# Weights in other pieces, on-chip copies of the sinks' v and other banks for four attention units, in a fused window-attention and gated-layer kernel

## The chip, the cores and the metric

The kernel runs on one core of a Trainium2 chip. Its five engines work side by side, each through its own list of instructions in order: TensorE (PE) multiplies matrices into PSUM, VectorE (DVE) and ScalarE (ACT) work elementwise, GpSimd (POOL) makes masks, casts and issues DMAs with a cast, SyncE (SP) issues other DMAs. Semaphores order them against each other. The metric is the device time of one launch in microseconds (us), the median of several runs; less is better.

## The reference

Attention first: q, k, v of 4 batches x 8 heads x 768 positions x 64, float32. A query sees the keys of a causal window of 128 positions and, besides, the first 4 positions (the sinks):

```python
keep = is_sink | in_window            # pos < 4, or 0 <= query - key < 128
scores = where(keep, q @ k.T / 8, -1e9)
a = softmax(scores);  attn = a @ v    # -> x of 3072 tokens x 512
```

Then a layer with a gate: h = x @ w_in (512 x 2048), g = h * sigmoid(beta * h), out = g @ w_out (2048 x 512), float32, 3072 x 512.

## The kernel before

The 3072 tokens are cut into 8 tiles (T) of 384. A tile's x needs four **units** of attention: unit n is one pair of heads and half a sequence, n // 8 its batch, n % 4 its pair of heads, n // 4 % 2 its half. Units 0 to 3 make tile 0, units 4 to 7 tile 1, and so on. A unit of the second half (4 to 7 among them) reads keys and sinks of the first half too.

A unit goes through these steps: q and k are loaded by SP as float32 (`load_qk`, L522), cast by POOL (`cast`, L621) and transposed by PE into bank tr, from where ACT or DVE copies them into qkT (`transpose_in`, L634, L641). Scores of the sinks are one matmul (`scores_sink`, L670) and an exponential on ACT (L673); scores of the window come in two groups, a and b, each with an exponential over two banks (`scores`, L700, L707) and a product with a mask on DVE (`apply_mask`, L714). `attend` multiplies with v (L759 the sinks' v in `v_sink`, L770 the window's v in `v_aug`), `normalise` divides by the sum (L779, L781), `transpose_out` turns the result through PE (L798) into xT (L802). Units 0 to 3 have the same steps with banks of their own. From unit 12 on (XBAR), q, k and v are landed with a cast by POOL's DMAs (L552, L561) and transposed by DMAs of SP (L567, L790).

The layer: a tile has 16 **blocks** of 128 columns of h. A block is four matmuls with w_in (`hidden`, L814), a tanh on ACT (L822) and a gate on DVE (L835); `project` (L843) multiplies g with w_out, 48 matmuls of a tile, for three tokens' groups t and 16 rows m of w_out, accumulating in acc0 or acc1; then out_sb is copied and stored (L851, L859). In tile 0 the blocks rotate through four banks, acc1, h0, h1 and acc0 among them, afterwards through h0 and h1.

PSUM has eight banks: s0, s1, tr and av (s_ps), h0 and h1 (h_ps), acc0 and acc1. In units 4 to 7 the sink scores go to s0, group a to s0 and s1, group b to h0 and h1, `attend` to av, `transpose_out` through tr.

The weights are loaded with a cast by POOL's DMAs: w_in in four pieces of 1 MB (`load_w_in`, L578; 0.5 MB each once cast), w_out in eight pieces (`load_w_out`, L583), v of tile 1 in three pieces (`load_v`, L542). The first four rows of k and v of all batches are loaded by `load_sinks`: k_rows early (L592), v_sink after the masks (L596).

**The order.** Each step is a node with a cost, and a planner (`Prog`) orders every engine's nodes: it takes, again and again, the node that can start first by its costs and by a model of the DMA queues, of equals the one that stands earlier in the program. Banks and buffers are reused in the order of the program: a node that writes one waits for all earlier readers. The resulting list of each engine is fixed, and the chip runs it in order. In the program, the main loop over s emits blocks (s < 16 for tile 0, then a gap of 8 steps, then a block per step), the units' steps by AGENDA (units 4 to 7: `in` at s = 0 to 3, the others from s = 16 on), casts, loads and projections (none for s < 16, three per step in the gap).

## Time and profile before

| | us |
|---|---|
| median of 3 runs | 228.73 (228.01 to 229.79) |
| the profiled execution | 228.59 |
| its span, first to last instruction | 226.9 |
| PE busy | 220.0 |
| ACT, DVE, POOL busy | 141.3, 132.6, 125.7 |
| first block of tile 0, of tile 1, of tile 2 | 17.32, 44.51, 70.53 |
| first projection | 35.08 |

The span is that of the profiled execution; 1.7 us lie around it. Times in the text are from the span's start. Matmuls are pipelined: each row gives a duration with a modelled end, and the next one often starts before it. Under the engines' names stand the lines of the kernel. A DMA's time runs from its issue to the landing of its last byte.

### The profile page before, as it was taken

To read this page: it belongs to the slowest core of one execution; us is meant where nothing else is said; L and a number is where in the kernel's file an instruction comes from. 1 tells how busy PE (TensorE), PEld (TensorE's weight loads), DVE (VectorE), ACT (ScalarE), POOL (GpSimd) and SP (SyncE) were. 2 spreads that over 40 slices of the span, in tenths; PEclk is the share of its full clock that TensorE was granted. 3 is DMA by queue.
4 is the path that set the end of the run, shared out by engine and by line. 5 is a ranking of instruction groups with operands and counts; after the bars stand their busy time and mean duration, and the time that the engine had idled before them with its cause. 6 is when DMAs were issued, how large, how long until landed. Compare 5 with 4: busy or idle time off the path is not lost.

```text
span 226.9 us, 4463 instructions
## 1 busy us (share of the span) xinstructions
PE 220.0 (97%) x1761; PEld 122.1 (54%) x1761; DVE 132.6 (58%) x264; ACT 141.3 (62%) x224; POOL 125.7 (55%) x191
## 2 busy tenths in 40 slices
PE   7999989999999999999999999999999999999995
PEld 4665545555555555555555555555555555555454
DVE  5466777488975776566565656555656564443200
ACT  1877796197586877566657766666656755555311
POOL 4689992899994979695939396876300000000000
PEclk9999999999999999999999999999999999999999
DMA  6999999999998999999999999998921012110122
GB/s 172 251 172 179 276 194 205 257 228 139 118 138 124 124 117 151 120 167 144 116 113 135 99 138 147 96 165 119 94 80 53 20 57 64 49 46 0 58 83 92
DMA packets 96901, 28.92 MB, mean 127 GB/s; under 512 B 83424, under 2 KB 93936, under 8 KB 96880
## 3 DMA queue, kind: packets, MB, share of 16 engines
q0 software_dynamic: 59232, 10.92, 65.7%
q1 hardware_dynamic: 34304, 16.79, 34.3%
q10 hardware_dynamic: 3344, 0.93, 1.9%
q8 instruction: 14, 0.23, 0.5%
q14 instruction: 7, 0.06, 0.1%
HBM read 27.34 MB, written 6.29 MB: 148 GB/s over the span
## 4 chain that ended last, share of the span: by engine, by line
PE 73%; DMA 15%; POOL 8%; issue 2%; SPq 1%; ACT 0%; POOLq 0%; ACTq 0%
PE acc L843 32%; PE h_ps L814 29%; DMA k_stage<-in_k_dram 8%; DMA w_out<-in_moe_w_out_dram 4%; PE s_ps L727 4%; PE s_ps L770 4%; POOL qk L621 3%; DMA w_in<-in_moe_w_in_dram 2%; POOL land L552 2%; PE h_ps L843 2%; POOL v_aug L561 1%; PE s_ps L759 1%; PE s_ps L670 1%; SPq L522 1%; POOL v_aug L532 0%
## 5 line engine op out<-in xcount | busy, mean ns | idle before, releaser
L822 ACT ACTIVATE th<-h_ps,beta_half 128x384 f32<-128x384 f32 x120 | 69.4, 581 | 59.7 <-PE h_ps L814 59.1
L843 PE MATMUL acc<-w_out,g 128*128 128x512 bf16 x368 | 99.7, 380 | 0.0
L814 PE MATMUL h_ps<-xT,w_in 128*128 128x384 bf16 x480 | 96.2, 326 | 0.0
L835 DVE SCALAR_TENSOR_TENSOR g<-th,h_ps 128x384 bf16<-128x384 f32 x120 | 65.6, 550 | 44.8 <-ACT th L822 44.0
L814 PEld LDWEIGHTS h_ps<-xT,w_in 128*128 128x128 bf16 x480 | 45.6, 98 | 39.8 <-issue 0.8
L843 PEld LDWEIGHTS acc<-w_out,g 128*128 128x128 bf16 x368 | 32.8, 98 | 28.8 <-issue 3.6
L552 POOL DMA_DIRECT2D land<-in_q_dram x40 | 30.2, 760 | 24.0 <-DVE rden L779 24.0
L552 POOL DMA_DIRECT2D land<-in_k_dram x40 | 30.3, 761 | 0.0
L561 POOL DMA_DIRECT2D v_aug<-in_v_dram x40 | 30.2, 760 | 0.0
L735 ACT ACTIVATE E<-s_ps 128x1536 bf16<-128x1536 f32 x20 | 28.8, 1442 | 0.0
L741 DVE TENSOR_TENSOR E<-E,mask 128x1536 bf16<-128x1536 bf16 x20 | 19.2, 958 | 16.4 <-ACT E L735 16.4
L851 ACT ACTIVATE out_sb<-acc 128x512 f32<-128x512 f32 x23 | 13.7, 596 | 7.6 <-PE acc L843 7.4
L770 PEld LDWEIGHTS s_ps<-v_aug,E 128*128 128x128 bf16 x336 | 15.2, 97 | 3.2 <-issue 1.2
L770 PE MATMUL s_ps<-v_aug,E 128*128 128x65 bf16 x336 | 16.8, 193 | 0.0
L707 ACT ACTIVATE E<-s_ps 128x768 bf16<-128x768 f32 x17 | 13.7, 811 | 4.3 <-PE s_ps L700 4.2
L781 DVE TENSOR_TENSOR o_norm<-s_ps,rden 128x384 bf16<-128x384 f32 x28 | 15.6, 556 | 0.8
L714 DVE TENSOR_TENSOR E<-E,mask 128x768 bf16<-128x768 bf16 x16 | 9.0, 572 | 2.0 <-ACT E L707 1.3
L727 PE MATMUL s_ps<-qkT 64*128 64x256 bf16 (+2 forms) x144 | 10.1, 254 | 0.0
L759 PE MATMUL s_ps<-v_sink,E_sink 128*128 128x130 bf16 x48 | 9.3, 219 | 0.0
L621 POOL CAST qk<-k_stage 128x384 bf16<-128x384 f32 x12 | 6.5, 544 | 4.7 <-DMA k_stage<-in_k_dram 4.4
L673 ACT ACTIVATE E_sink<-s_ps 128x384 bf16<-128x384 f32 x16 | 7.8, 490 | 1.5 <-PE s_ps L670 1.5
L727 PEld LDWEIGHTS s_ps<-qkT 64*128 64x128 bf16 x144 | 4.9, 94 | 7.1 <-issue 5.8
(75 smaller groups left out, 155.2 us busy)
## 6 DMA issues: line engine op xcount, KB each, us to landing
out_dram<-out_sb SPq DMA_DIRECT2D x23, 256.0 KB, 2.7
q_stage<-in_q_dram SPq DMA_DIRECT2D x12, 192.0 KB, 7.4
k_stage<-in_k_dram SPq DMA_DIRECT2D x12, 192.0 KB, 7.9
w_in<-in_moe_w_in_dram POOLq DMA_DIRECT2D x4, 512.0 KB, 6.8
w_out<-in_moe_w_out_dram POOLq DMA_DIRECT2D x8, 256.0 KB, 9.6
land<-in_q_dram POOLq DMA_DIRECT2D x40, 48.0 KB, 3.7
land<-in_k_dram POOLq DMA_DIRECT2D x40, 48.0 KB, 4.0
v_aug<-in_v_dram POOLq DMA_DIRECT2D x40, 48.0 KB, 3.4
```

The source lines that it names most:

```text
L552: op("gp", lambda e, d=d, s=s: e.dma_start(d, s), w=[("land", pb, half, x, hh)], after=after, dma=f"l{pb}{half}{x}{hh}", **transfer(TT * D ...
L561: op("gp", lambda e, d=d, s=s: e.dma_start(d, s), w=[("v", pb, 3 * half + c, hh) for c in range(3)], after=after, dma=f"lv{pb}{half}{hh}", ...
L707: op("act", lambda e: e.activation(both, src[:, :, 0:TT], AF.Exp, bias=0.0, scale=SCALE), x=list(names), w=[("E", n % NE, c)], **act(768))
L727: op("pe", lambda e, at=at, w=w, kb=kb, qb=qb, nq=nq, hh=hh, rows=rows, bank=bank: e.matmul(s_ps[:, 2 * hh + bank, at:at + w], keys_of(pb, ...
L735: op("act", lambda e: e.activation(E[z][:, :, :], src, AF.Exp, bias=0.0, scale=SCALE), x=list(S_NAMES), w=[("E", z, 0), ("E", z, 1)], **ac ...
L741: op("dve", lambda e: e.tensor_tensor(E[z][:, :, :], E[z][:, :, :], m.unsqueeze(1).to_broadcast([128, 2, 768]), ALU.mult), r=[("E", z, 0), ...
L770: last=(x == len(kbs) - 1): e.matmul(av_ps[:, at + hh * D1:at + hh * D1 + D1], E[z][:, hh, col:col + 128], v_aug[:, pb, hh, kb, 0:D1], sta ...
L781: op("dve", lambda e: e.tensor_tensor(o_norm[o][:, :, :, :].rearrange("p m h d -> p (m h) d"), src[:, :, 0:D], rden[z][:, :].unsqueeze(2). ...
L814: op("pe", lambda e: e.matmul(bank, w_in16[:, c, m * 128:(m + 1) * 128], xT[:, c, T * TT:(T + 1) * TT], start=(c == 0), stop=(c == 3)), r= ...
L822: op("act", lambda e: e.activation(th[i % 3][:, :], bank, AF.Tanh, bias=0.0, scale=beta_half[:, m:m + 1]), x=[name], r=["beta"], w=[("th", ...
L835: op("dve", lambda e: e.scalar_tensor_tensor(g[T % 2][:, m, :], th[i % 3][:, :], 1.0, bank, ALU.add, ALU.mult), r=[("th", i % 3)], x=[name ...
L843: op("pe", lambda e: e.matmul(bank[:, 0:width], g[T % 2][:, m, t * 128:(t + 1) * 128], w_out16[:, m, cols], start=(m == 0), stop=(m == NM ...
```

## The change

- w_in comes in pieces of 1, 1 and 2 MB: blocks 8 to 15 read the third.
- The sinks' v is no longer loaded at once by two DMAs. For batch 0 and batch 1, DVE copies the four rows out of v_aug (`sink_values`); for batches 2 and 3, POOL loads them later (`load_sink_values`, two DMAs each, at s = 48 and 80). v_sink's dependences are kept by batch.
- POOL's first piece of w_out stands ahead of the three pieces of v of tile 1; the other pieces of w_out come at s = 1 and 2.
- Units 4 to 7 leave AGENDA. Their casts and transposes stand at s = -2 to 1, with ACT for the copy of unit 5 alone (before: 5 and 7). Their other steps stand in `second_units`, ahead of s = 16: sink scores in av (units 4, 5) and tr (6, 7), group a in s0 and s1, group b in h0 and h1, `attend` of units 4 and 5 in av, of 6 in s0 and of 7 in s1; `transpose_out` through tr or av, copied by DVE for unit 4 and by ACT for 5 to 7 (before: DVE for all).

```diff
@@ -41,6 +41,9 @@
 KINDS = ("aaattw", "wtwttw")
 
 
+SECOND_ACT = (5,)
+
+
 XBAR = 12
 
 NEG = -1.0e6
@@ -54,9 +57,6 @@
 FIRST = {8: 23, 9: 26, 10: 28, 11: 31}
 FIRST.update({n: 18 + 4 * (n - 8) for n in range(12, NU)})
 AGENDA = {}
-for n in range(4, 8):
-    for step, at in (("in", n - 4), ("sink", 16), ("a", 16), ("b", 16), ("av", 17), ("out", 18)):
-        AGENDA.setdefault(at if step == "in" else at + 1 * (n - 4), []).append((n, step))
 for n in range(8, NU):
     for at, step in STEPS.items():
         AGENDA.setdefault(FIRST[n] + at, []).append((n, step))
@@ -584,17 +584,28 @@
            w=[("w_out", mm) for mm in range(m, m + ms)],
            dma=f"wo{m}", **transfer(ms * 128 * NOUT * 4, 416, 740.0, 3.0))
 
-    def load_sinks(x, after=()):
+    def load_sink_keys(after=()):
+        for hh in range(2):
+            src = k[:, :, 0:NSINK, :].rearrange("b (g h) s d -> h (b g) s d", h=2)[hh]
+            op("gp", lambda e, hh=hh, src=src: e.dma_start(k_rows[:, :, hh, :], src),
+               w=[("k_rows", hh)], after=after, dma=f"sk{hh}", busy=650.0, lag=300.0, weight=0.4)
+
+    def sink_values(b, eng, after=()):
+
         for hh in range(2):
             rows = slice(HEAD1 * hh, HEAD1 * hh + NSINK)
-            if x:
-                src = k[:, :, 0:NSINK, :].rearrange("b (g h) s d -> h (b g) s d", h=2)[hh]
-                op("gp", lambda e, hh=hh, src=src: e.dma_start(k_rows[:, :, hh, :], src),
-                   w=[("k_rows", hh)], after=after, dma=f"sk{hh}", busy=650.0, lag=300.0, weight=0.4)
-            else:
-                src = v[:, :, 0:NSINK, :].rearrange("b (g h) s d -> s h (b g) d", h=2)[:, hh]
-                op("gp", lambda e, rows=rows, hh=hh, src=src: e.dma_start(v_sink[rows, :, hh, 0:D], src),
-                   w=[("v_sink", hh)], r=["v_sink"], after=after, dma=f"sv{hh}", busy=650.0, lag=400.0, weight=0.4)
+            op(eng, lambda e, rows=rows, hh=hh: e.tensor_copy(
+                v_sink[rows, 4 * b:4 * b + 4, hh, 0:D], v_aug[0:NSINK, :, hh, 0, 0:D]),
+               r=["v_sink", *(("v", z, 0, hh) for z in range(4))], w=[("v_sink", b, hh)],
+               busy=200.0, lag=140.0, after=after)
+
+    def load_sink_values(b):
+        for hh in range(2):
+            rows = slice(HEAD1 * hh, HEAD1 * hh + NSINK)
+            src = v[b, :, 0:NSINK, :].rearrange("(g h) s d -> s h g d", h=2)[:, hh]
+            op("gp", lambda e, rows=rows, hh=hh, src=src: e.dma_start(
+                v_sink[rows, 4 * b:4 * b + 4, hh, 0:D], src),
+               w=[("v_sink", b, hh)], r=["v_sink"], after=[("rden", 0)], dma=f"sv{b}{hh}", busy=650.0, lag=400.0, weight=0.4)
 
     def sink_keys():
 
@@ -665,14 +676,14 @@
     def queries_of(pb, rows, qb, nq):
         return qkT[pb][rows, qb // 3, 0, qb % 3 * 128:(qb % 3 + nq) * 128]
 
-    def scores_sink(n):
+    def scores_sink(n, bank=s_ps[:, 0, :], name="s0"):
         pb = place(n)[3]
-        op("pe", lambda e: e.matmul(s_ps[:, 0, 0:TT], k_sink[:, n // 8 * 4 + n % 4, :],
+        op("pe", lambda e: e.matmul(bank[:, 0:TT], k_sink[:, n // 8 * 4 + n % 4, :],
                                     queries_of(pb, slice(0, 128), 3, 3), start=True, stop=True),
-           r=["k_sink", ("k_sink", 0), ("k_sink", 1), ("qkT", pb, 1)], w=["s0"], **pe(TT))
-        op("act", lambda e: e.activation(E_sink[n % NE][:, :], s_ps[:, 0, 0:TT], AF.Exp, bias=0.0,
+           r=["k_sink", ("k_sink", 0), ("k_sink", 1), ("qkT", pb, 1)], w=[name], **pe(TT))
+        op("act", lambda e: e.activation(E_sink[n % NE][:, :], bank[:, 0:TT], AF.Exp, bias=0.0,
                                          scale=SCALE),
-           x=["s0"], w=[("E_sink", n % NE)], **act(TT))
+           x=[name], w=[("E_sink", n % NE)], **act(TT))
 
     def keys_read(pb, half, runs):
         return [("qT", pb), *(("qkT", pb, x) for x in sorted({half, *(kb // 3 for kb, _, _ in runs)}))]
@@ -760,7 +771,7 @@
                         av_ps[:, at:at + 2 * D1], E_sink[z][:, mm * 128:mm * 128 + 128],
                         v_sink[:, n // 8 * 4 + hp, :, :].rearrange("p h e -> p (h e)"),
                         start=True, stop=False, skip_group_check=True),
-                       r=[("E_sink", z), "v_sink", ("v_sink", 0), ("v_sink", 1)], w=[name],
+                       r=[("E_sink", z), "v_sink", ("v_sink", n // 8, 0), ("v_sink", n // 8, 1)], w=[name],
                        **pe(130))
                 for hh in range(2):
                     kbs = range(m + 1) if half == 0 else (m - 1, m)
@@ -876,7 +887,7 @@
     load_w_in(0, 4, [("v", 0, 0, 0)])
     cast_v(1)
     cast(2)
-    load_sinks(1, [("v", 1, 0, 0)])
+    load_sink_keys([("v", 1, 0, 0)])
 
     select(ident32[:, :], ones32[:, :], [[1, 32]], ALU.is_equal, 0.0, 0, -1, ["ones32"], ["ident32"])
     transpose_first(0)
@@ -895,9 +906,8 @@
     cast(3)
     load_w_in(4, 4, [("k16", 0)])
     cast_v(2)
-    load_w_in(8, 4, [("v", 2, 0, 0)])
+    load_w_in(8, 8, [("v", 2, 0, 0)])
     cast_v(3)
-    load_w_in(12, 4, [("v", 3, 0, 0)])
     for n in range(4):
         if n < 2:
             transpose_first(n + 2)
@@ -909,10 +919,10 @@
                     load_qk(y, x, [("w_in", 0, 4)])
             fill("gp", k_sink[:, :, :], 0.0, ["k_sink"], busy=1800.0, after=[("v", 3, 0, 0)])
             masks([("v", 3, 0, 0)])
-            load_sinks(0, [("v", 3, 0, 0)])
+            sink_values(0, "dve")
+            load_w_out(0, 2, [("v", 3, 0, 0)])
             for c in range(3):
                 load_v(1, c, [("v", 3, 0, 0)])
-            load_w_out(0, 2, [("v", 3, 0, 0)])
         bank = (acc[1], "acc1") if n < 3 else (h_ps[:, 0, :], "h0")
         attend(n, *bank)
         normalise(n, *bank)
@@ -926,8 +936,7 @@
     sink_keys()
 
 
-    casts = {-1: 4, 0: 5, 1: 6, 2: 7}
-    casts.update({FIRST[n] - 2: n for n in range(8, XBAR)})
+    casts = {FIRST[n] - 2: n for n in range(8, XBAR)}
     lands, lands_v, turns = {}, {}, {}
     for n in range(XBAR, NU):
         lands[FIRST[n] - 14] = n
@@ -935,7 +944,30 @@
         turns[FIRST[n] - 4] = n
     todo = [(0, x % 2, x // 2) for x in range(2 * NM)] + [(0, 2, m) for m in range(NM)]
     todo += [(T, t, m) for T in range(1, NT) for t in range(3) for m in range(NM)]
+
+    def second_units():
+
+        for n in range(4, 8):
+            scores_sink(n, *(((av_ps, "av"), (tr_ps, "tr"))[n // 6]))
+            for c in range(2):
+                scores(n, c, (("s0", "s1"), ("h0", "h1"))[c])
+                apply_mask(n, c)
+            if n > 5:
+                attend(n - 2)
+                normalise(n - 2)
+        for n in range(4, 8):
+            if n > 5:
+                bank = s_ps[:, n - 6, :], f"s{n - 6}"
+                attend(n, *bank)
+                normalise(n, *bank)
+            transpose_out(n, *((tr_ps, "tr"), (av_ps, "av"))[n % 2], "dve" if n == 4 else "act")
+
     for s in range(-2, S_END + NM):
+        if s == NM:
+            second_units()
+        if s < 2:
+            cast(s + 6)
+            transpose_in(s + 6, eng="act" if s + 6 in SECOND_ACT else "dve")
         i = block_of(s) if 0 <= s < S_END else None
         if i is not None:
             hidden(i, 3 if i < 2 else 0)
@@ -943,7 +975,7 @@
         for n, step in AGENDA.get(s, ()):
             half = place(n)[2]
             if step == "in" and n < XBAR:
-                transpose_in(n, eng="act" if n in (5, 7) else "dve")
+                transpose_in(n)
             if step == "sink" and half == 1:
                 scores_sink(n)
             if step == "b" and n >= XBAR:
@@ -951,10 +983,7 @@
                 later.append(lambda n=n: mask_at_once(n))
             if step in ("a", "b") and n < XBAR:
                 c = "ab".index(step)
-                if n < 8 and c == 1:
-                    scores(n, c, ("h0", "h1"))
-                else:
-                    scores(n, c, ("s0", "s1"))
+                scores(n, c, ("s0", "s1"))
                 later.append(lambda n=n, c=c: apply_mask(n, c))
             if step == "av":
                 attend(n)
@@ -965,7 +994,7 @@
                 transpose_out(n)
         if s in casts:
             cast(casts[s])
-        if s == 0:
+        if s == 1:
             for m in range(2, 8, 2):
                 load_w_out(m, 2, [("w_in", 0, 0)])
         if s == 2:
@@ -978,6 +1007,10 @@
                 load_v(2, c, [("w_out", 2 * c + 6)])
         if s == 23:
             load_v(2, 2)
+        if s == 34:
+            sink_values(1, "dve", [("rden", 1)])
+        if s in (48, 80):
+            load_sink_values(2 if s == 48 else 3)
         if s in lands:
             for x in range(2):
                 land_qk(lands[s], x, [("rden", 0)])
```

## The prediction

> **What bounds the kernel now.** I read the busy line first, then the slices, then stretches of the first 60 us by engine, then the order of TensorE's work there with the landings.
>
> ```profile
> PE 220.0 (97%) x1761; PEld 122.1 (54%) x1761; DVE 132.6 (58%) x264; ACT 141.3 (62%) x224; POOL 125.7 (55%) x191
> PE   7999989999999999999999999999999999999995
> ...
> 17.30:22.50 5.20, 5.20 (x35) 3.07 (x34) 3.32 (x7) 4.00 (x9) 5.20 (x16) 1.00 1.14 176
> 22.50:25.40 2.90, 2.83 (x18) 1.47 (x15) 2.42 (x6) 2.58 (x5) 2.90 (x4) 1.00 1.14 290
> 25.40:29.90 4.50, 4.16 (x33) 2.42 (x33) 3.65 (x7) 3.06 (x6) 4.38 (x9) 1.00 1.49 237
> 29.90:35.10 5.20, 3.89 (x52) 1.96 (x50) 4.09 (x8) 5.20 (x9) 4.50 (x8) 1.00 1.55 196
> 35.10:44.50 9.40, 9.40 (x97) 5.43 (x96) 5.91 (x15) 3.67 (x6) 4.89 (x7) 1.00 1.25 234
> 44.50:60.00 15.50, 14.84 (x128) 8.26 (x127) 12.65 (x25) 11.51 (x19) 15.05 (x23) 1.00 1.70 167
> ```
>
> The columns of the stretches are length, then busy time of PE, weight loads, DVE, ACT and POOL, then clock, DMA share and GB/s. PE is the bound: after 60 us it never idles. Every matmul of the first layer, of the second layer and of the attention is the same before and after, so **the end moves only by the idle time of PE before 60 us**. That is 0.07 + 0.34 + 1.31 + 0 + 0.66 = 2.4 us from 17.3 us on. A modelled matmul end (0.33 us for a 128x384 matmul that is followed 0.16 us later by the next) hides up to 0.16 us at each gap; with some eight gaps in 25 to 35 us, the idle of that stretch is 1.65 by the rows and about 2.9 in truth. Idle before 17.3 us belongs to the first four units, which this change hardly touches.
>
> ```profile
> 21.91 1.46 PE L814 MATMUL acc<-xT,w_in 128*128 128x384 bf16 x8
> 23.21 1.46 PE L814 MATMUL h_ps<-xT,w_in 128*128 128x384 bf16 x8
> 24.51 1.76 PE L814 MATMUL acc<-xT,w_in 128*128 128x384 bf16 x8
> ...
> 34.81 0.34 PE L700 MATMUL h_ps<-qkT 64*128 64x128 bf16 x4 [0.36 <-ACT E L707]
> 35.08 0.39 PE L843 MATMUL acc<-w_out,g 128*128 128x512 bf16 x1
> ```
>
> (Order of PE's work.) A block is four matmuls, 0.65 us. Counted from 17.3 us, the row of 21.91 is blocks 7 and 8, that of 24.51 blocks 11 and 12. Block 8 starts at 22.56. Block 12 wants the last quarter of w_in: its row takes 1.76 where the others take 1.46, a wait of 0.3. The first matmul of the second layer comes at 35.08.
>
> ```profile
> w_in<-in_moe_w_in_dram POOLq DMA_DIRECT2D x1, 512.0 KB, 7.9
> ...
> w_in<-in_moe_w_in_dram POOLq DMA_DIRECT2D x1, 512.0 KB, 9.8
> ...
> w_out<-in_moe_w_out_dram POOLq DMA_DIRECT2D x1, 256.0 KB, 10.0
> ```
>
> (DMA issues of short windows, us to landing last.) The third piece of w_in is issued at 14.02 and lands at 21.9; the fourth, issued at 15.57, at 25.4, which is where block 12 goes on. The first piece of w_out, issued at 24.85, lands at 34.9, just ahead of 35.08.
>
> **The change part by part.**
>
> *w_in in 1, 1 and 2 MB.* POOL issues one DMA less (0.74 us of POOL). But blocks 8 to 11, which now start on the piece that landed at 21.9, must wait for the whole 2 MB, and nothing stands ready on PE: unit 4's k lands at 26.2 (issued 18.37, 7.8 us), and the projections need banks that the blocks still hold. Landing, bounded from both sides: undisturbed, from the second piece's landing (12.45 + 5.5 = 17.95) at the pace of the w_out pieces later (24.85 + 10.0 and 26.67 + 9.4 are 1.25 us apart for 256 KB), 1,024 KB take 5.0 us: 22.95, a wait of 0.4. With the sharing as it is now, 25.4: 2.85. Until 22 us queue 0 moves nearly alone; the q and k loads of units 4 to 7 (issued from 17.96) share after that. The rows of the new piece are twice as long, so I expect it to hold a larger part of the engines than now: 24.5, a wait of 1.95. The wait of 0.3 at block 12 goes: **+1.65**.
>
> The Trainium skill (DMA: Bandwidth & Descriptors, Anatomy of one DMA) counts about 2.0 us fixed per DMA and, in its rules for authors, asks for 1 MiB or more per transfer. By that the merged piece would land 2.0 us earlier, at 23.4, and the term would be +0.55. The rows speak against it: w_out pieces queued behind each other land 1.25 us apart, so a fixed part is hidden already.
>
> *w_out's first piece ahead of v, sinks' v off POOL.* POOL's issues after the masks fall by 0.74 + 1.29 (two DMAs of sinks' v). Its first w_out piece goes out at 24.85 - 0.74 - 1.29 - 2.68 (three v DMAs that now come after) = about 20.2 and stands in queue 0 right behind w_in: landing about 27 instead of 34.9. The accumulators are free when block 15 is gated, about 31; then m = 0 and 1 of two row tiles, four projections of 0.22 us, can fill gaps before 35. The v pieces are pushed back by that 1.25 us and gain what the sinks' two transfers held; v's third piece landed at 33.6 (23.98 + 9.6) and attention of unit 4 went on at 33.68. I keep it at 33 to 34.9.
>
> *Sinks' v copied by DVE.* Two copies of 4x256 bf16 at about 15.3, two more at block 26. No such row: bounds 0.07 (memset of 4x16 in the same tile) and 0.35 (128x384 copy of xT); I take 0.2, nearest in elements to a small fixed cost plus half of that copy. The first two may stand between DVE's reciprocal (15.24) and its products (15.47, 16.45) and delay xT, and so the first block, by 0.4. The wait at block 8 swallows this, since a DMA sets it; without that wait it costs 0.4. The other two run while DVE is 82% busy and PE has work of its own: nothing. Batches 2 and 3 cost POOL four DMAs of 0.65 us at blocks 40 and 72; what is queued behind them are the landing loads of units some 14 blocks ahead, which land 2.4 to 4 us after their issue: nothing.
>
> *Units 4 to 7 on other banks.* Now a unit's sink scores and half of its other scores take turns on bank s0, so the exponentials go on to 41 us. With the sinks on av and tr, ACT is held by itself alone: 4 x (0.39 + 2 x 0.70) = 7.2 us at the pace of its starts today (30.32, 30.71, 31.40), and one copy of qkT (0.80) goes from ACT to DVE (0.96; DVE has 4.09 of 5.20 busy there). Unit 7's xT should come at about 40 instead of 44.4 (its copy today: 44.06, 0.36 us). That alone buys nothing, as PE is busy 9.40 of 9.40 from 35.1 on. It buys what can be done before 35, where PE was idle for 2.9 us: four projections (0.86), one or two sink scores (0.16 each), a group of scores (0.27) and perhaps one attention (0.5) can move in. Sum 1.8 to 2.0: **-1.9**, between 0 (they find no place in PE's fixed order) and -2.9.
>
> *44.5 to 60 us.* PE waits 0.66 there, all of it for POOL.
>
> ```profile
> PE s_ps L634 <- POOL qk L621: 0.7, 2, 0.5
> ```
>
> (Waits of PE in that stretch: us, times, longest.) Casts of units 8 to 11 wait behind landing loads on POOL, 97% busy. Their q and k are asked for when pieces of w_out land, about a microsecond earlier after the change, and PE will have the second tile's blocks at hand from 40 us. I take half of it: **-0.3**, between -0.66 and +0.6 (PE's order is fixed by a planner, and a cast that comes late stops it).
>
> **Sum.** 1.65 - 1.9 - 0.3 = -0.55. The profiled execution took 228.59 (span 226.9 and 1.7 around it), 0.14 under the median of the runs: **228.0**. One per cent, 2.3 us, is about what a measurement of this kernel can tell from no change, so this is within it.
>
> **The rivals.**
>
> 1. *The wait is not paid back* (slower). Place: PE at block 8. Price: the 2 MB land at 25.4 or later, +2.55; block 15 then ends past 31, tanh and gates of blocks 8 to 15 fall on ACT and DVE together with the exponentials and masks of units 4 to 7 (ACT already 5.20 of 5.20), and what moves into the gaps shrinks from 1.9 to 0.5 or less. +2.0 to +2.6: 230.6 to 231.2. It decides once the piece lands after 25. For it: the last quarter lands at 25.4 today. Against it: 0.72 of the 1.02 MB seem to have moved by 22 (third piece landed at 21.9). Chance 0.15.
> 2. *The early w_out piece does nothing.* The accumulators are held by the blocks until 31, only four projections exist, v's later landing holds the attention of units 4 and 5 to 34.9, and POOL's casts stay as they are. Then -1.9 becomes -0.6 and -0.3 becomes 0: +1.05, 229.6. That the change doesn't do what it says is this case. Chance 0.22.
> 3. *The piece lands early and all gaps close* (faster). Landing 23.2, a wait of 0.65 less the 0.3; -2.4 before 35, -0.5 later: -2.55, 226.0. For it: the undisturbed pace. Against: q and k share the engines from about 21 us on (their first landing, 25.2, took 7.3 us). Chance 0.18.
> 4. *The pause slows PE.* At the start, two 128x384 matmuls took 0.82 us (3.23) and later 0.50 (9.42), so one took 0.32 instead of 0.16; PE was slow from 1.2 to about 6.5. If a pause as long as the wait brings that back, blocks 8 to 15 lose up to half of some 4 us: +2.0 on the forecast, 230.0. No pause in the trace is longer than 0.5 us once PE is fast, and the granted clock reads 1.00 throughout. Chance 0.04. The Trainium skill (TensorE: Matmul & The Clock Gate, Part 1) has the array fall to half rate after an idle window of about 3.4 us; by it the wait that I expect is too short, and only a landing past 26 would bring this case.
>
> **How the numbers follow.** The forecast, 227.0 to 229.2 around 228.0, has 0.41; the rivals have the chances above. Faster by over 1% (below 226.4) is two thirds of rival 3 and a little of the forecast's edge, 0.15. Slower by over 1% (above 231.0) is some two thirds of rival 1 and part of rivals 2 and 4 where v or casts are later still, 0.15. Within 1%: 0.70. The range goes from 226.2, inside rival 3, to 230.9, inside rival 1.
>
> **What would show it.** Right: block 8 about 2 us after block 7, ended by a DMA of w_in; the first projection before 35, near 31; the second tile's first block at about 40 instead of 44.5; PE's idle of 25.4 to 35.1 down from 1.65 to 0.8 or less; nothing changed after 70 us but a shift. Wrong: no pause at block 8 (then add 1.5 us of gain), or new pauses of PE between 35 and 70 us, where I count on projections and blocks to fill everything, or a first block that moves by more than 0.4 us.

## The result and the profile after

The changed kernel takes **230.1 us** (median of 22 runs, 228.65 to 232.7) against 228.72 us for the kernel before in as many runs beside it (227.58 to 230.84). The ratio is **1.0062**, 95% interval 1.0042 to 1.0083: slower by 0.6%, 1.4 us, where 0.3% faster was forecast. The profiled execution took 230.91 us (span 229.2). Ratios leave out runs that took over 1.5% more than the fastest of their kernel: here the one of 232.7 us, in e5_before_2mb below two of nine.

Line numbers have moved: blocks of the first layer are L825 (L814 before), projections L854 (L843), transposes of q and k L645 (L634), casts L632 (L621), copies of qkT L652 (L641). L597 is the new copy of the sinks' v.

Busy line and PE's slices of the changed kernel:

```profile
PE 219.9 (96%) x1734; PEld 122.7 (54%) x1761; DVE 134.4 (59%) x266; ACT 141.4 (62%) x226; POOL 126.9 (55%) x192
...
PE   7998799999999999999999999999999999999995
```

PE's work is the same (219.9 us for 220.0); the trace lacks 27 of 1,761 matmul records, all of projections, so some small gaps read after 34 us are false. The fifth slice (22.9 to 28.7 us) has fallen to 7. Stretches of the changed kernel, with the columns of the forecast (length; busy time of PE, weight loads, DVE, ACT, POOL; clock; DMA share; GB/s):

```profile
17.30:22.50 5.20, 4.53 (x53) 3.05 (x50) 3.20 (x10) 2.66 (x8) 5.20 (x16) 1.00 1.03 166
22.50:25.40 2.90, 2.90 (x18) 1.49 (x16) 2.63 (x6) 2.65 (x5) 2.05 (x3) 1.00 1.10 250
25.40:29.90 4.50, 2.97 (x22) 1.74 (x22) 2.48 (x6) 2.41 (x5) 3.79 (x7) 1.00 1.32 240
29.90:35.10 5.20, 4.95 (x45) 2.98 (x43) 4.40 (x8) 4.59 (x9) 4.22 (x8) 1.00 1.62 209
35.10:44.50 9.40, 9.29 (x119) 5.53 (x119) 7.94 (x19) 7.27 (x13) 4.14 (x6) 1.00 1.23 230
44.50:60.00 15.50, 14.85 (x123) 7.92 (x122) 11.79 (x23) 10.74 (x19) 14.71 (x22) 1.00 1.54 165
```

PE idles 0.67 us in the first stretch and 1.53 in the third, and the granted clock is 1.00 throughout in this execution. In 29.9 to 35.1 us there is less idle time than before; PE arrives there late. Order of PE's work of the changed kernel (start, us, operation, idle time before it and what ended it):

```profile
19.10 0.34 PE L809 MATMUL s_ps<-ident,o_norm 128*128 128x128 bf16 x3 [0.62 <-DVE xT L813]
...
20.05 0.33 PE L825 MATMUL acc<-xT,w_in 128*128 128x384 bf16 x1
...
24.64 0.81 PE L825 MATMUL acc<-xT,w_in 128*128 128x384 bf16 x4
26.67 0.34 PE L645 MATMUL s_ps<-ident,qk 128*128 128x128 bf16 x3 [1.22 <-POOL qk L632]
26.85 0.81 PE L825 MATMUL acc<-xT,w_in 128*128 128x384 bf16 x4
...
34.67 0.38 PE L854 MATMUL acc<-w_out,g 128*128 128x512 bf16 x1
...
45.65 0.81 PE L825 MATMUL h_ps<-xT,w_in 128*128 128x384 bf16 x4
```

Two things are new. The first block starts at 20.05 instead of 17.32; 1.90 us of that is this execution's start (attention of unit 3 begins at 17.53 instead of 15.63), the other 0.83 lies between that attention and the block. And block 7, begun at 24.64, is followed by no block until 26.85. The wait isn't charged to w_in: what ends it is the cast of unit 4's q.

Order of work on POOL and DVE of the changed kernel:

```profile
15.85 1.81 POOL L444 MEMSET k_sink<- 128x2048 bf16 x1
15.89 2.08 DVE L597 COPY v_sink<-v_aug 4x256 bf16<-4x256 bf16 x2
17.99 0.20 DVE L790 RECIPROCAL rden<-acc 128x6 f32<-128x6 f32 x1
18.22 0.56 DVE L792 TENSOR_TENSOR o_norm<-acc,rden 128x384 bf16<-128x384 f32 x1
18.70 0.35 DVE L813 COPY xT<-s_ps 128x384 bf16<-128x384 bf16 x1
...
26.11 0.50 POOL L632 CAST qk<-q_stage 128x384 bf16<-128x384 f32 x1 [1.57 <-DMA q_stage<-in_q_dram]
```

Two copies of 4 rows take 2.08 us while POOL's fill of k_sink runs beside them, and the normalisation that leads to xT stands behind them on DVE. Lower, the cast that PE waits for has itself waited 1.57 us for q.

### The profile page after: what moved, and what is told of

It is laid out like the page before. It is cut to its first block, busy times and chain, and to the rows that moved or that the text cites. A ratio compares the mean times of both kernels' runs of the same rounds, so it can differ in the third digit from the quotient of the medians.

```text
span 229.2 us, 4446 instructions
## 1 busy us (share of the span) xinstructions
PE 219.9 (96%) x1734; PEld 122.7 (54%) x1761; DVE 134.4 (59%) x266; ACT 141.4 (62%) x226; POOL 126.9 (55%) x192
## 4 chain that ended last, share of the span: by engine, by line
PE 71%; DMA 17%; POOL 8%; issue 2%; SPq 1%; ACT 0%; DVE 0%; POOLq 0%; ACTq 0%
PE acc L854 31%; PE h_ps L825 29%; DMA k_stage<-in_k_dram 6%; DMA w_out<-in_moe_w_out_dram 5%; PE s_ps L781 4%; PE s_ps L738 4%; DMA q_stage<-in_q_dram 3%; DMA w_in<-in_moe_w_in_dram 2%; POOL land L552 2%; POOL qk L632 2%; PE h_ps L854 2%; POOL v_aug L561 1%; PE s_ps L770 1%; PE s_ps L681 1%; SPq L522 1%
## 5 line engine op out<-in xcount | busy, mean ns | idle before, releaser
L825 PE MATMUL h_ps<-xT,w_in 128*128 128x384 bf16 x480 | 96.8, 326 | 0.4 <-DVE g L846 0.2
L854 PE MATMUL acc<-w_out,g 128*128 128x512 bf16 x341 | 94.5, 380 | 1.2 <-issue 0.2
L825 PEld LDWEIGHTS h_ps<-xT,w_in 128*128 128x128 bf16 x480 | 46.1, 98 | 40.3 <-issue 0.3
L854 PEld LDWEIGHTS acc<-w_out,g 128*128 128x128 bf16 x368 | 33.0, 98 | 28.8 <-issue 4.1
L632 POOL CAST qk<-k_stage 128x384 bf16<-128x384 f32 x12 | 6.5, 542 | 5.8 <-DMA k_stage<-in_k_dram 5.8
L652 DVE COPY qkT<-s_ps 128x768 bf16<-128x768 bf16 x7 | 6.7, 953 | 4.0 <-PE s_ps L645 3.9
```

Of the source, the lines that this page charges most:

```text
L825: op("pe", lambda e: e.matmul(bank, w_in16[:, c, m * 128:(m + 1) * 128], xT[:, c, T * TT:(T + 1) * TT], start=(c == 0), stop=(c == 3)), r= ...
L854: op("pe", lambda e: e.matmul(bank[:, 0:width], g[T % 2][:, m, t * 128:(t + 1) * 128], w_out16[:, m, cols], start=(m == 0), stop=(m == NM ...
```

## The experiments

The expectations name the theories by letters. **A**: the 2 MB piece holds up block 8, and the slow copies hold up the first block; the two lie in series and cover each other. **B**: the copies alone are the loss. **C**: the loss comes from units 4 to 7, behind tile 0. Letters beyond these stand for what the text beside them says. Ratios are to the kernel before, run beside each kernel, with 95% intervals.

**Copies on ACT** (e1_act)

```
-            sink_values(0, "dve")
+            sink_values(0, "act")
```

> The changed kernel with the first batch's two copies of the sinks' v on ACT instead of DVE; nothing else. Theory A (two delays in series in tile 0: the copies hold DVE for 2.08 us at 15.9, and the 2 MB piece of w_in lands at 25.4 to 25.9): the reciprocal of unit 2 follows its attention within 0.2 us again, the first block comes 1 to 2 us earlier against attention of unit 3, but block 8 still waits for the landing, so the end gains at most 0.8 us: 229.3 to 230.1. Theory B (the copies alone are the loss): the whole loss of 1.4 us goes, 228.7. Theory C (the loss comes from units 4 to 7, behind tile 0): no change, 230.1.

231.11 us; 1.0095 (1.0059 to 1.0132). The copies take 404 and 412 ns on ACT, the first block comes 1.68 us after unit 3's attention begins, as before the change, and nothing is won: block 8 starts at 27.09. B falls. (A had 230.1 at most: the time is a miss.)

**w_in in four pieces of 1 MB, all else as changed** (e2_four, again as f2_four_again)

```
-    load_w_in(8, 8, [("v", 2, 0, 0)])
+    load_w_in(8, 4, [("v", 2, 0, 0)])
+    load_w_in(12, 4, [("v", 3, 0, 0)])
```

> The changed kernel with w_in in four pieces of 1 MB as before; nothing else. Theory A: no wait at block 8; POOL's memset of k_sink starts 0.75 us later, behind the fourth piece's issue, so the copies on DVE may get through ahead of it; gain 1.5 to 2.5 us, 227.6 to 228.6. Theory B: gain below 0.5 unless the copies got through. Theory C: no change, 230.1.

> The changed kernel with w_in in four pieces, once more: 0.2 to 0.8 us faster than before, ratio 0.9965 to 0.9990.

227.78 us, 0.9976 (0.9955 to 0.9998), and on another chip 227.79, 0.9986 (0.9953 to 1.002). Splitting that one DMA takes 0.86% off the changed kernel (1.0062 less 0.9976), 2.0 us; by the second measurement 0.76%, 1.7 us. C falls. It also puts an issue between v and the fill, which ends the copies' trouble. Order on POOL and DVE of the first of these:

```profile
15.54 0.45 DVE L597 COPY v_sink<-v_aug 4x256 bf16<-4x256 bf16 x2
15.81 0.74 POOL L578 DMA_DIRECT2D w_in<-in_moe_w_in_dram  x1 [0.30 <-POOL v_aug L532]
16.54 1.82 POOL L444 MEMSET k_sink<- 128x2048 bf16 x1
```

The copies take 215 and 221 ns, and are over before the fill starts. No wait stands ahead of block 8.

**The two together** (e3_act_four: four pieces, and copies on ACT)

> The changed kernel with w_in in four pieces and the first two copies on ACT. Theory A: both delays gone, 1.5 to 2.8 us faster than the changed kernel, 227.3 to 228.6, and at most 0.3 faster than with four pieces alone if the copies there got through ahead of the memset. Theory C (units 4 to 7 lose): stays above 229.5.

228.04 us; 0.9984 (0.996 to 1.0008). Not told apart from four pieces alone.

**The fill of k_sink at 3 us instead of 16** (e4_memset_early on the changed kernel, e6_four_memset on four pieces)

```
+    fill("gp", k_sink[:, :, :], 0.0, ["k_sink"], after=["add_t2", "ident32"])
...
-            fill("gp", k_sink[:, :, :], 0.0, ["k_sink"], after=[("v", 3, 0, 0)])
```

> The changed kernel with POOL's memset of k_sink at 3 us, where POOL idles until 5 us; nothing else. If the copies took 1.83 us because the memset of 1.81 us ran beside them on POOL, they now take 0.2 to 0.5 us each and the first block comes 1.5 to 2 us earlier against attention of unit 3. If a copy of four partitions is slow by itself, they still take about 2 us together. The end: by theory A the landing of w_in at block 8 takes most of it, 228.9 to 230.0; w_out's first issues move up by 1.8 us on POOL, which may give up to 0.5 more.

> The changed kernel with w_in in four pieces and POOL's memset of k_sink at 3 us. Theory A: w_out's first issues and the masks come 1.8 us earlier on POOL; since queue 0 is busy with w_in until 25 us, the landings hardly move, and the end stays within 0.5 us of four pieces alone: 227.3 to 228.3. Theory E (POOL's issues bound tile 1's weights): another 0.5 to 1.0 us faster, 226.8 to 227.3.

230.16 us, 1.0071 (1.0043 to 1.0099); with four pieces 229.37, 1.0048 (1.0019 to 1.0076), outside both of the ranges expected. Order of work of the first (POOL, DVE and PE):

```profile
3.02 1.80 POOL L444 MEMSET k_sink<- 128x2048 bf16 x1
...
15.57 0.45 DVE L597 COPY v_sink<-v_aug 4x256 bf16<-4x256 bf16 x2
...
26.32 0.34 PE L645 MATMUL s_ps<-ident,qk 128*128 128x128 bf16 x3 [2.19 <-POOL qk L632]
26.50 0.81 PE L825 MATMUL acc<-xT,w_in 128*128 128x384 bf16 x4
```

The same two copies, on the same engine, take 0.45 us once the fill runs elsewhere: the fill is their cause. The first block comes 1.69 us after unit 3's attention begins, instead of 2.52, and the wait at block 8 is longer, 2.19 for 1.22: the one delay had covered the other. As a price this pair is not clean, since the moved fill costs four pieces some 0.7%, and what that comes from wasn't followed up.

**The piece of 2 MB alone, in the kernel before** (e5_before_2mb)

```
-    load_w_in(8, 4, [("v", 2, 0, 0)])
+    load_w_in(8, 8, [("v", 2, 0, 0)])
-    load_w_in(12, 4, [("v", 3, 0, 0)])
```

> The kernel before with the last two pieces of w_in as one of 2 MB; nothing else. Theory A (the merged piece is the loss): block 8 waits 1.5 to 3 us for a landing at 25.4 to 26, the end is 1.3 to 2.3 us later than before: 230.0 to 231.0. Theory D (the merged piece costs only where it meets the copies and the order of units 4 to 7): below 0.6 us, 228.2 to 229.2.

230.74 us (median of the seven runs that count); 1.0084 (1.0049 to 1.0119), 1.9 us. PE's order in the profiled execution, the longest of the nine at 233.04 us:

```profile
24.17 0.81 PE L814 MATMUL acc<-xT,w_in 128*128 128x384 bf16 x4
27.58 0.34 PE L634 MATMUL s_ps<-ident,qk 128*128 128x128 bf16 x3 [2.60 <-POOL qk L621]
27.76 1.30 PE L814 MATMUL acc<-xT,w_in 128*128 128x384 bf16 x4
28.86 1.49 PE L814 MATMUL h_ps<-xT,w_in 128*128 128x384 bf16 x4
```

No copies here, and the full pause. Of the 18 profiles, the four with the 2 MB piece and unit 4's transposes in the old place have 2.21 to 3.59 us from the start of block 7 to that of block 8; the other fourteen have 0.65. Put in alone or taken out alone, the piece is worth 1.7 to 2.0 us.

The rows show a second thing. Blocks 8 and 9 take 1.10 and 1.28 us to the next start, not 0.65. A stretch of this execution, with the columns as above (the clock stands third from the end):

```profile
28.00:29.00 1.00, 1.00 (x5) 0.50 (x4) 0.00 (x0) 0.00 (x0) 1.00 (x3) 0.50 1.43 236
```

The granted clock is 0.50 here; the trace's clock record has it from 27.93 us on for 3.41 us, just behind the pause, and at 1.00 before and after.

**Units 4 to 7 alone; copies and early piece alone** (e7_units: the changed kernel with four pieces, sinks' v by DMA and v ahead of w_out; e8_order: the kernel before with the copies and w_out's first piece ahead of v)

```
-            sink_values(0, "dve")
-            load_w_out(0, 2, [("v", 3, 0, 0)])
+            load_sink_v([("v", 3, 0, 0)])
...
+            load_w_out(0, 2, [("v", 3, 0, 0)])
```

> Of the changed kernel only units 4 to 7 on other banks; w_in in four pieces, the sinks' v by two DMAs, v ahead of w_out as before. Theory A (PE's gaps before 35 us are closed only where projections are at hand): first projection at 34 to 35 us, idle time of PE in 25 to 35 us as before, 0 to 0.4 us faster than before: 228.2 to 228.7. My sum in the prediction would have 1.0 us or so of its 1.9 here: 227.5.

> The kernel before with the sinks' v copied on chip and w_out's first piece ahead of v; w_in in four pieces, units 4 to 7 as before. Theory A: the first w_out piece lands at 28 to 29, first projection near 30, two copies of 0.2 us each on DVE ahead of POOL's memset; 0.3 to 0.8 us faster than before: 227.8 to 228.4. My sum in the prediction would have 0.9 us for the four projections: 227.7.

228.8 us, 1.001 (0.9984 to 1.0036), and 229.55, 1.004 (1.0013 to 1.0068). Neither half gains, though the two together do by a little (four pieces, 0.9976 and 0.9986); e8_order lies far from the gain expected. In e7_units a new wait of PE gives back part (waits of PE from 80 to 100 us; us, times, longest):

```profile
PE h_ps L832 <- DMA xT<-o_norm: 1.1, 1, 1.1
```

In the profile of e8_order the second piece of w_in landed at 21.1 instead of 17.9, and PE stops 1.60 us for unit 4's q at 27.48. Whether its other eleven runs did so isn't known, and what its 0.4% come from stays open.

**The kernel before, twice more** (e9_before_look, e12_before_look2)

> The kernel before once more, for its profile. If the first profile of it began unusually early (first block at 17.32, attention of unit 0 at 10.29, where the other kernels' profiles have 10.6 to 12.5), this one's first block comes 0.3 to 2 us later while w_in, q and k land at nearly the same times; PE's idle time from 25.4 to 35.1 is then 0.5 to 1.2 instead of 1.65, and the time from the first block to the end 0.5 to 1.5 us shorter than 206.9. If the start is no cause, both stay: 1.65 and 206.9.

> The kernel before a third time, for its profile: as the second, another draw of the start. Two profiles of one kernel that begin apart tell whether the end moves by as much as the first block does (nothing lies in between) or by less (the landings hold the middle).

228.03 and 229.11 us. The idle time that the forecast lived on is there in each: 1.65, 1.74 and 1.62 us in 25.4 to 35.1. The 206.9 us from the first block to the end of PE's work became 205.8 and 206.7: in the first of the two this half of the expectation came, but not through the idle time that it named. The 0.66 of 44.5 to 60 us is not there. Stretch of the first, then of the second:

```profile
44.50:60.00 15.50, 15.50 (x137) 8.59 (x135) 12.82 (x26) 11.51 (x19) 15.45 (x25) 1.00 1.70 183
```

```profile
44.50:60.00 15.50, 15.34 (x133) 8.46 (x132) 12.06 (x25) 11.26 (x19) 15.50 (x25) 1.00 1.71 188
```

**Pieces of 1, 1, 0.5 and 1.5 MB, in the kernel before** (e10_split)

```
-    load_w_in(8, 4, [("v", 2, 0, 0)])
-    load_w_in(12, 4, [("v", 3, 0, 0)])
+    load_w_in(8, 2, [("v", 2, 0, 0)])
+    load_w_in(10, 6, [("v", 3, 0, 0)])
```

> The kernel before with w_in in pieces of 1, 1, 0.5 and 1.5 MB: as many DMAs, but blocks 10 to 15 (not 12 to 15) read the last. Theory A (blocks wait for the whole piece that they read): a wait of 1 to 2 us at block 10, the end 0.5 to 1.3 us later than before, between before and one piece of 2 MB (1.9 later): 229.2 to 230.0. If the loss of the 2 MB piece came from POOL issuing one DMA less, or from its size alone: no change, 228.7.

228.42 us; 1.0000 (0.9975 to 1.0025). A miss: I expected a loss. In its profile the last piece lands at 24.87 and block 10 starts at 25.57 without a wait. Here a large piece cost nothing, as the blocks before it lasted until it landed. That profile shows one thing more: its first block comes at 19.02, 1.70 us later than in the profile of the kernel before, and PE's last matmul ends at 224.21 for 224.19. What lies between was held by something that did not come later, probably the landings.

**Two pieces of w_out ahead of v, with four pieces of w_in** (e11_wout2)

```
-            load_w_out(0, 2, [("v", 3, 0, 0)])
+            for m in (0, 2):
+                load_w_out(m, 2, [("v", 3, 0, 0)])
```

> The changed kernel with w_in in four pieces and two pieces of w_out ahead of v instead of one. For: four more projections are at hand by 31 us, where PE idles 1.1 us in 30 to 35: up to 0.7 us faster than with one, 227.1 to 227.8. Against: v lands 1.25 us later and attention of units 4 and 5 with it, 36 instead of 34.8: 0 to 0.8 us slower, 227.8 to 228.6. I expect 227.6.

229.22 us; 1.0002 (0.9973 to 1.0032): a miss. More weights early is no gain either.

**Block 8 ahead of unit 4's transposes** (f1_block8_first on the changed kernel; g1_block8_act, with the copies on ACT; f3_blocks_four, with four pieces)

```
-        if s < 2:
-            cast(s + 6)
-            transpose_in(s + 6, ...)
+        if 9 <= s < 13:
+            cast(s - 5)
+            transpose_in(s - 5, ...)
```

Unit 4's transposes are held until block 8 is done.

> The changed kernel, 2 MB piece and all, with the casts and transposes of units 4 to 7 later in the program and unit 4's transposes held behind block 8 on PE. If the landing alone sets the price: block 8 starts at the landing, 25.4 to 25.9, and the end stays at 230.1 within 0.3, since unit 4's transposes merely change places with it. If the order adds to it: 0.5 to 1.0 us faster, 229.1 to 229.6. In both the kernel stays slower than before (228.7).

> As f1 (2 MB piece, block 8 ahead of unit 4's transposes), with the first two copies of the sinks' v on ACT. If the two delays cover each other: the first block comes at 17.3 to 19.5 with no stop for DVE's xT, block 8 waits 0.5 to 2 us for w_in's landing at 24.2 to 25.9, and the end is between four pieces (227.8) and the changed kernel (230.1): 228.6 to 229.5, faster than f1 by 0.3 to 1.0. If the landing costs nothing once the order is mended: 227.8. If it holds the whole price: 229.6 or more.

> Four pieces of w_in, and unit 4's transposes behind block 8 (the planner then runs blocks 8 to 15 through and the transposes after them). If PE's stops for bank tr behind transposes (1.1 us in 30 to 35 us with four pieces alone) are what kept the rest of the gain away: 0.3 to 0.9 us faster than four pieces alone, 227.0 to 227.5. If units 4 to 7 bound tile 1 and start later by this: equal or slower, 227.8 to 228.8.

229.63 us, 1.0064 (1.0036 to 1.0091); 229.91, 1.0049 (1.0019 to 1.008); 228.91, 1.0007 (0.9978 to 1.0037), no gain over four pieces alone. PE's order in the first:

```profile
18.71 0.34 PE L809 MATMUL s_ps<-ident,o_norm 128*128 128x128 bf16 x3 [1.90 <-DVE xT L813]
...
19.66 0.65 PE L825 MATMUL acc<-xT,w_in 128*128 128x384 bf16 x3
...
24.25 1.46 PE L825 MATMUL acc<-xT,w_in 128*128 128x384 bf16 x8
```

Blocks 7 and 8 now run on end, in a kernel that still has the 2 MB. But this execution's attention began 1.8 us earlier (10.43 for 12.22), v came later than DVE was ready for it, and the copies delay the first block by 2 us. With that delay the piece is there in time. On ACT (g1) the delay is gone, and the gain of 0.0015 lies within the intervals. So with this order the 2 MB still cost 0.4 to 0.6% (f1 and g1 against f3); what that rest consists of, their profiles don't show. The profile of f1 is the fastest of its twelve runs (228.87 us), and five of the twelve have a mean granted clock of 0.991 to 0.993, so others may have stopped where it didn't.

## Why the prediction was wrong, point by point

**w_in, +1.65: the wait was right, its size a little short, and the clock left out.** The runs have 1.7 to 2.0 us by the two ways of measuring it. The piece (issue of a short window, us to landing last) landed later than the 24.5 that I took:

```profile
w_in<-in_moe_w_in_dram POOLq DMA_DIRECT2D x1, 1024.0 KB, 11.3
```

Issued at 14.53, it is there at about 25.9; the others with the old order have 25.4 to 26.7. Only f1 and g1 came near, with 24.2 and 24.6. The undisturbed pace was no bound worth having, and the 2.0 us that the Trainium skill (DMA: Bandwidth & Descriptors, Anatomy of one DMA) counts as fixed per DMA were not saved: two pieces in one landed no earlier than two had landed (25.4 before). The step also missed that PE's order puts unit 4's transposes ahead of block 8. So a second landing had to come, q at about 26.05 with its cast of 0.50, and block 8 started 0.95 after its weights. My sign to look for, a wait ended by a DMA of w_in, was therefore never there; the wait was.

Part of these 1.7 to 2.0 us is my fourth rival, "The pause slows PE", which I gave 0.04. In e5_before_2mb an idle stretch of 2.6 us brought the half clock back, shorter than the 3.4 us that I quoted; the landing there, at 26.7, was past the 26 that I asked for. It doesn't always come: after 1.22 us in the changed kernel's profile and 2.19 in that of e4_memset_early a block takes its 0.65. But it comes often. Half clock for 3.41 us lowers the mean granted clock of a run from 1.00 to 0.993, and a mean of 0.993 or less was measured in:

| | runs |
|---|---|
| the changed kernel | 12 of 22 |
| the same with e1, e4 and e5 (2 MB piece, unit 4's transposes in the old place) | 22 of 45 |
| the changed kernel with four pieces, six versions | 1 of 72 |
| the kernel before, beside the experiments | 10 of 126 |

The changed kernel's ten runs at full clock have a median of 229.88 us, the others that count 230.38. Against 228.72 us before, the runs at full clock still lose 1.2, so the wait is most of the loss, and the clock adds about half a microsecond in every second run. Where it fell in the runs without a profile is not recorded.

**Copies of the sinks' v, 0.2 us each: wrong by ten, and yet without effect on the sum.** View of the copy's line in the changed kernel (ns: shortest, median, longest):

```profile
L597 DVE COPY v_sink<-v_aug x4: 207/374/1834, 15.9 to 60.5; 4x256 bf16<-4x256 bf16 x4
```

0.2 us was right for a copy by itself: the first pair takes 215 to 225 ns each where no fill runs beside it. (One of the later pair takes 0.4 to 0.5 us in eight of the profiles, which wasn't followed up.) My bounds, 0.07 and 0.35, were durations of DVE alone; the price came from POOL, and the change itself moved the fill there, since one issue of 0.74 us less stood ahead of it. The delay of 0.83 was swallowed at block 8, as I had said of my 0.4 (e1 and e4 remove it and gain nothing). Where the wait is gone, I held that a delay costs 0.4. That isn't shown: in f2_four_again the first block comes 2.18 us after unit 3's attention begins, in e2_four 1.68, and the two executions took 227.67 and 227.75 us.

**Units 4 to 7 and the early piece, -1.9: this is the step that failed and turned the sign.** With the 2 MB out, all the rest of the change is worth 0.24 and 0.14%, 0.3 to 0.55 us, for 2.2 forecast in this term and the next. The four projections did find their place. PE's order with four pieces (f2_four_again):

```profile
29.59 0.60 PE L854 MATMUL acc<-w_out,g 128*128 128x512 bf16 x2
...
31.27 0.60 PE L854 MATMUL acc<-w_out,g 128*128 128x512 bf16 x2
32.50 0.51 PE L645 MATMUL s_ps<-ident,qk 128*128 128x128 bf16 x6 [0.62 <-ACT qkT L652]
...
34.05 0.51 PE L645 MATMUL s_ps<-ident,qk 128*128 128x128 bf16 x6 [0.45 <-DVE qkT L652]
```

But PE's stops stayed, and other work came later. Matmuls that start from 25.4 to 35.1 us, by kind, in traces with all records:

| | blocks | transposes | scores | attention | projections |
|---|---|---|---|---|---|
| before, three profiles | 16, 18, 20 | 24, 24, 24 | 26, 24, 18 | 15, 15, 15 | 1, 0, 0 |
| four pieces (f2) | 20 | 24 | 22 | 9 | 4 |

Each matmul taken at the median time of its shape from its start to the next (0.216 us for a projection, 0.163 for one of a block), PE does 6.95 us of work in this stretch, where the three profiles of before have 6.40, 6.34 and 6.38: 0.6 us more, of the 1.9 forecast. Two stretches of the same kernel, to be held against the same two of the kernel before:

```profile
25.40:29.90 4.50, 4.20 (x30) 2.33 (x29) 3.88 (x8) 3.28 (x7) 4.50 (x8) 1.00 1.28 249
29.90:35.10 5.20, 4.12 (x53) 2.19 (x52) 3.54 (x7) 4.92 (x9) 3.99 (x7) 1.00 1.69 194
```

Idle time is 0.30 + 1.08 = 1.38, where the three profiles of before have 1.62 to 1.74; my sign was 0.8 or less. I had treated idle time as room that ready work fills. Much of it is the pace of a chain on other engines: landing, cast, transpose, copy of qkT, scores, exponentials. PE's largest stops are now at transposes that want a bank back from the copies of qkT (0.62 and 0.45 above). And the change itself made the chain later at its head. POOL's work in f2, then in the kernel before:

```profile
24.86 0.51 POOL L632 CAST qk<-q_stage 128x384 bf16<-128x384 f32 x1 [0.16 <-DMA q_stage<-in_q_dram]
25.30 2.14 POOL L583 DMA_DIRECT2D w_out<-in_moe_w_out_dram  x3
27.42 0.54 POOL L632 CAST qk<-k_stage 128x384 bf16<-128x384 f32 x1
```

```profile
25.54 0.56 POOL L621 CAST qk<-q_stage 128x384 bf16<-128x384 f32 x1
26.21 0.51 POOL L621 CAST qk<-k_stage 128x384 bf16<-128x384 f32 x1
26.67 0.70 POOL L583 DMA_DIRECT2D w_out<-in_moe_w_out_dram  x1
```

Unit 4's k landed at 25.72 in f2, at 26.16 before; yet three issues of w_out stand between the two casts, and k is cast 1.2 us later than before. They stand there in e2_four and in the changed kernel too, and not in e7_units, where v is ahead of w_out. Unit 4's attention then starts at 34.77, against 33.26, 33.56 and 34.44 in the three profiles of before and 33.68 in e7_units; unit 7's k is cast at 33.37 instead of 31.92. I had counted POOL's fewer issues as a gain and never asked which of them would stand ahead of a cast. What these issues cost at the end no run prices: e7_units, without them, gains nothing either. The lower end that I gave, 0, is nearly what happened, but for another reason than mine: the projections found their place.

The banks did what I said of ACT (the last exponential starts at 37.93 instead of 40.28), but the second tile's first block moved from 44.51 only to 43.40, not to 40: the last xT is copied at about 42. In the changed kernel that block comes at 45.65.

**44.5 to 60 us, -0.3: taken from one execution.** The 0.66 was 0 and 0.16 in the two other profiles of the kernel before. There was little to gain.

**Sum.** By e5_before_2mb the piece costs 1.9 us, and by four pieces the rest gives back 0.3 to 0.55: 1.35 to 1.6 against the 1.4 measured and the -0.55 forecast. Of the rivals, "The wait is not paid back" has the landing, after 25, though its 230.6 to 231.2 us lay half a microsecond or more too high. The small return is nearer to "The early w_out piece does nothing", with its -0.6 and its attention of unit 4 at 34.9: without any pause, in four pieces, the return is as small, so it doesn't need the crowding on ACT and DVE that the first rival gave as a reason. "The pause slows PE" is there in part, as said above. My range holds the time thanks to the rivals, not to the forecast, whose sign was wrong. One of my signs of error was met, a first block moved by more than 0.4. Of the signs of being right three weren't: the first projection near 31 (34.67 is the first recorded, and the weights of an earlier one are loaded at 33.9), the second tile's first block at 40, and the idle time down to 0.8 (1.78).

**A version that beats both**, if barely: four pieces of w_in with the rest of the change, 0.24 and 0.14% under the kernel before. The interval of the first measurement lies below 1, that of the second holds it.

## What to carry to other kernels

The size of a DMA sets when its first consumer may start: merging two pieces saved one issue of 0.74 us on an engine that wasn't the bound, and made four blocks wait for bytes of later ones. A pause of PE can cost more than its length, if the clock falls behind it. Before pricing idle time as room for other work, find the chain that makes it, and ask what the change puts ahead of that chain on the other engines: here three issues of weights between two casts. And when an instruction goes from a queue, look at what moves up behind it, and at what then runs side by side.

## What the runs showed of the hardware

**A DVE copy that waits out a POOL fill.** A bf16 copy of 4x256 on DVE took 1,834 ns with POOL's 1.81-us memset of 128x2048 bf16 beside it, and 215 to 225 ns in the same place without; on ACT, beside the memset, 404 and 412. The Trainium skill (SBUF — State Buffer, Who interferes with whom) says that DVE and GpSimd share one pair of ports, that a copy in a two-port mode needs it, and that whoever issues first holds it for its whole instruction; the memset started at 15.85, the copy at 15.89, and the copy lasted just beyond the memset's end. The trace agrees. In f1_block8_first the copy's row starts 0.03 us ahead of the memset's, at 15.43, and it still took 1,903 ns, to 0.06 beyond the memset's end; so rows that begin this close don't tell which of the two will wait.

**A pause that brought the half clock back.** In e5_before_2mb PE stood still for 2.6 us, from 24.98 to 27.58; from 27.93 on the granted clock was 0.50 for 3.41 us, and a matmul of 128x384 took 0.32 us to the next start instead of 0.163. After pauses of 1.22 and 2.19 us in two other profiles it stayed at 1.00.

**Two groups of starts.** Attention of unit 0 begins at 10.3 to 10.9 us in eight profiles and at 11.6 to 12.5 in the other ten, the same code (four pieces) in both: 11.64 and 10.70. In the late ones PE's early matmuls keep twice their duration longer; two of 128x384 for the masks take 0.82 us still at 10.83 in the changed kernel, and 0.50 at 9.42 before. The clock records of the ten late traces begin, with 1.00, at 10.8 to 12.2 us, those of six of the early ones at 6.1 to 9.2 (two have none); before that the stretches read 1.00 without a record. It costs little at the end (227.75 and 227.67 us for that pair), and the issues of w_in don't move with it (the last at 15.81 and 15.97). Why the full clock comes at two times wasn't found.

**A late piece.** In five of the profiles the second piece of w_in landed at 20.6 to 21.5 us instead of 17.9 to 19.7, and the fourth piece at 26.4 to 27.2 instead of 25.1 to 25.8. In two of the five (e3_act_four and e8_order) PE then stops 1.90 and 1.60 us for unit 4's q, which landed at 27.39 and 26.87, although w_in comes in four pieces. One profile is a draw from such starts, so single profiles differ by more than the effect looked for here, and sums made from one profile's idle time inherit that.
